# Reordering the first loads of an attention kernel, and one transpose ahead of a step's scores

## The chip, the cores and the metric

The kernel runs on one core of a Trainium2 chip. The metric is the device time of one execution in microseconds (us); lower is better. Most executions agree within 0.3%. All times inside an execution are us from the start of its span.

## The reference

```python
xn = layernorm(x)                                   # x: 1 x 2048 x 512
q  = (xn @ wq)                                      # 32 heads of 128
p  = softmax(q @ k_cache.T * 128**-0.5)             # 2048 keys a head
s  = (p @ v_cache) @ wo
g  = silu(relu(xn @ w1 + b1)**2 @ w2 + b2)
out = x + s * g
```

## The kernel before

The tensor engine (PE) does the matmuls and some transposes (its weight loads are listed as PEld), ACT the exponentials, DVE and POOL the rest; SP sends nearly all transfers. Queries are taken in four blocks of 512, which are four tiles of 128 rows each. Block 0, head 0 has a start of its own: K of head 0 comes as two plain halves that PE transposes, each x tile is normalised, transposed on PE and projected, and scores are made tile by tile, so that ACT can begin early. A step of head 0 is one tile of queries against one half of the keys: its scores (queries times K), its exponential, and its PV (the exponentials times V).

```python
def ln_load(j, i, eng=SP):      # x tile i of block j: 128 KB
    t_xl[jt] = S.emit_dma(eng, partial(_dma, out=x_ln[:, i, :], in_=...), sl_xl[i], deps=[...])

def load_k0(b):                 # half b of K, head 0: 256 KB, by SP
    ...
def k0_transpose(b):            # 8 PE transposes; waits for that half
    ...
def first_transpose(i):         # 4 PE transposes of normalised tile i
    ...
def first_proj(i):              # 4 matmuls with wq of head 0
    ...
# --- the loads, in program order of each engine ---
ln_load(0, 0, SP)
ln_load(0, 1, AC)
load_k0(0)
fill_wq(0, AC)                  # wq of head 0: 128 KB in rows of 256 bytes
load_k0(1)
E(AC, partial(_act, out=th_t[:, 0, 0:1], in_=warm[:, 0:1], func=ACT.Exp), deps=[t_warm])
ln_load(0, 2, SP)
ln_load(0, 3, SP)
fill_wq(1); load_v0(0); load_v0(1)
...
# --- the work, in program order of each engine ---
warm_up(36)
k0_transpose(0); k0_copy(0)
ln_bn(0, 0); ln_rstd(0, 0, eng=DV); ln_bn(0, 1); ln_scale(0, 0)
first_transpose(0)
k0_transpose(1); k0_copy(1)
...
first_copy(0); first_proj(0); ...
first_transpose(1)
gen_scores(0); ...              # gen_scores and gen_pv are steps of head 0
gen_pv(0)
ln_bn(0, 3, 0, HD)
gen_scores(2)
ln_scale(0, 2)
first_transpose(2)
ln_bn(0, 3, HD, D)
gen_scores(3)
first_copy(2)
...
```

PE works strictly in this order: the first x transposes stand behind the transposes of K's first half, and the first projection behind those of K's second half.

The softmax here doesn't subtract the row's maximum and nothing guards it: scores larger than these inputs give would overflow.

## Time and profile before

| | before |
|---|---|
| time, median of the 3 runs | 1238.17 us (1237.9 to 1238.31) |
| span of the profiled execution | 1236.1 us |
| first scores start | 7.58 us |
| weights of head 1's first scores start | 16.59 us |
| from there to the end | 1219.5 us |

The prediction shows the busy table, the chain of waits and the issue rows. The timeline of PE, with columns start, duration, engine, line, operation, tiles, count, and in brackets the idle time before it and what ended that:

```profile
4.86 0.73 PE L196 MATMUL psO<-ident,kT 128*128 128x128 bf16 x8
...
5.95 0.61 PE L196 MATMUL psO<-ident,kT 128*128 128x128 bf16 x8
6.72 0.38 PE L152 MATMUL psF<-xnT,wq_sb 128*128 128x128 bf16 x4 [0.16 <-DVE xnT L179]
```

The reader is to see that the projection waits for the copy of the x tile. The view of transfers, cut to the issue of each K half (last column: us from issue to landing):

```profile
kT<-in_A_k_cache_dram SPq DMA_DIRECT2D x1, 256.0 KB, 3.6
...
kT<-in_A_k_cache_dram SPq DMA_DIRECT2D x1, 256.0 KB, 4.2
```

Issued at 1.18 and 1.64, the halves land at 4.82 and 5.85. The first is not early enough, though the timeline shows no wait: it counts the last warm-up matmul as busy until 5.00. That matmul starts at 4.69, and the warm-up matmuls start 0.107 apart, so the transposes could have started at 4.80. They start at 4.86, which is 0.046 after the landing, as they do within 0.001 in twelve of the fourteen traces. That cost nothing yet: they end near 5.43, and PE then waits for the normalised x tile until 5.71. Nor does the second set hold anything: it ends near 6.40, and the projection starts at 6.72. An estimate from these starts: the first half could have come 0.29 later, and the second 0.37 later, before tile 0 had to wait for K.

### The profile page before, as it was taken

Reading aid. Unit: us, or ns where it says so; the run is one execution under the profiler, and the core shown is the slowest. Engines: PE = TensorE matmul, PEld = TensorE weight load, DVE = VectorE, ACT = ScalarE, POOL = GpSimd, SP = SyncE. Lnnn points to the kernel's source line nnn. Section 1 sums busy time; section 2 is a strip of 40 time slices with the busy share of each in tenths; the row PEclk is TensorE's granted clock in tenths of the full one; section 3 lists DMA queues with packets and bytes.
Section 4 is the critical chain, followed back from the end, with each engine's and each line's share of the span. In section 5 each row is a group of like instructions: output and inputs, shape, how many; then the busy total and the mean of one; then the engine's idle time right before and its main releaser. Section 6 shows DMA issues by size and latency. Waiting matters only on the chain.

```text
span 1236.1 us, 26728 instructions
## 1 busy us (share of the span) xinstructions
PE 1220.8 (99%) x11678; PEld 819.1 (66%) x11885; DVE 472.8 (38%) x953; ACT 1054.6 (85%) x1044; POOL 32.0 (3%) x73
## 2 busy tenths in 40 slices
PE   9999999999999999999999999999999999999998
PEld 7666666666666666666666666666666666666665
DVE  4453323244435332334444532333344333324333
ACT  7888888888888888888888888888888888888885
POOL 1010000000002000000000200000000000000000
PEclk9999999999999999999999999999999999999999
DMA  9999998787879897768779878787778788878771
GB/s 211 203 245 194 187 178 134 130 144 143 140 152 171 144 158 129 141 138 144 133 135 169 171 138 144 141 148 133 134 146 148 146 154 158 137 134 146 145 124 31
DMA packets 686868, 185.41 MB, mean 150 GB/s; under 512 B 673536, under 2 KB 685568, under 8 KB 686752
## 3 DMA queue, kind: packets, MB, share of 16 engines
q1 hardware_dynamic: 684656, 179.62, 80.0%
q0 software_dynamic: 1424, 3.81, 1.2%
q8 instruction: 94, 1.54, 0.6%
q10 hardware_dynamic: 672, 0.26, 0.1%
q14 instruction: 22, 0.18, 0.0%
HBM read 96.60 MB, written 2.10 MB: 80 GB/s over the span
## 4 chain that ended last, share of the span: by engine, by line
PE 98%; issue 1%; DVE 0%; DMA 0%; POOL 0%; DVEq 0%
PE psO L157 38%; PE psA L152 35%; PE psF L152 25%; PE psA L157 0%; DMA x_ln<-in_A_x_dram 0%; DVE out_t L165 0%; PE psF L196 0%; DVE tmp_t L175 0%; PE psO L152 0%; DVE xnT L179 0%; DVE st_t L200 0%; POOL rstd L165 0%; DVE xn_t L171 0%; DVE mv_t L204 0%; DVE ve_t L171 0%
## 5 line engine op out<-in xcount | busy, mean ns | idle before, releaser
L161 ACT ACTIVATE pT<-psA 128x1024 bf16<-128x1024 f32 x1024 | 1044.5, 1024 | 162.9 <-PE psA L152 117.6
L157 PEld LDWEIGHTS psO<-v_sb,pT 128*128 128x128 bf16 x8192 | 547.9, 98 | 240.3 <-issue 12.4
L157 PE MATMUL psO<-v_sb,pT 128*128 128x129 bf16 x8192 | 631.2, 220 | 0.5
L152 PE MATMUL psA<-qt_sb,kT 128*128 128x512 bf16 x1840 | 562.9, 379 | 10.1
L179 DVE COPY o_un<-psO 128x258 f32<-128x258 f32 x256 | 97.4, 422 | 399.5 <-PE psO L157 398.8
L152 PE MATMUL psF<-xnT,wq_sb 128*128 128x512 bf16 (+1 forms) x508 | 165.7, 374 | 0.4 <-DVE xnT L179 0.2
L152 PE MATMUL psF<-wo_all,oT 128*128 128x512 bf16 x478 | 163.2, 379 | 0.1
L152 PEld LDWEIGHTS psA<-qt_sb,kT 128*128 128x128 bf16 x2032 | 157.0, 98 | 0.0
L179 DVE CAST qt_sb<-psF 128x512 bf16<-128x512 f32 (+1 forms) x130 | 88.0, 677 | 97.3 <-PE psF L152 93.7
L165 DVE TENSOR_TENSOR o_bf<-o_un,rden 128x512 bf16<-128x512 f32 x128 | 88.6, 692 | 4.7 <-DVE rden L183 0.3
L152 PEld LDWEIGHTS psF<-xnT,wq_sb 128*128 128x128 bf16 x520 | 50.3, 98 | 60.0 <-issue 0.3
L171 DVE TENSOR_SCALAR r_t<-psF,b1f 128x512 bf16<-128x512 f32 x56 | 42.0, 750 | 117.4 <-PE psF L152 117.4
L152 PEld LDWEIGHTS psF<-wo_all,oT 128*128 128x128 bf16 x480 | 46.9, 98 | 56.4
L152 PE MATMUL psF<-xnT,w_sb 128*128 128x512 bf16 x224 | 77.1, 379 | 0.0
L152 PE MATMUL psF<-w_sb,h2T 128*128 128x512 bf16 x223 | 73.7, 379 | 0.0
L152 PEld LDWEIGHTS psF<-xnT,w_sb 128*128 128x128 bf16 x224 | 21.9, 98 | 26.4
L152 PEld LDWEIGHTS psF<-w_sb,h2T 128*128 128x128 bf16 x224 | 21.9, 98 | 26.4
L165 DVE TENSOR_TENSOR z_t<-psF,b2bc 128x512 f32<-128x512 f32 x16 | 11.1, 692 | 67.2 <-PE psF L152 62.0
L165 DVE TENSOR_TENSOR acc<-psF,acc 128x512 f32<-128x512 f32 x28 | 19.3, 689 | 30.0 <-PE psF L152 30.0
L208 POOL DMA_DIRECT2D out_dram<-out_t x12 | 6.7, 554 | 891.1 <-DVE out_t L165 891.1
L165 DVE TENSOR_TENSOR h2T<-r_t 128x512 bf16<-128x512 bf16 x56 | 23.8, 426 | 1.9
L183 DVE RECIPROCAL rden<-o_un 128x4 f32<-128x4 f32 x128 | 22.9, 179 | 4.4
(47 smaller groups left out, 165.2 us busy)
## 6 DMA issues: line engine op xcount, KB each, us to landing
v_sb<-in_A_v_cache_dram SPq DMA_DIRECT2D x127, 512.0 KB, 4.7
wq_sb<-in_A_wq_dram SPq DMA_DIRECT2D x127, 128.0 KB, 3.1
wo_all<-in_A_wo_dram SPq DMA_DIRECT2D x4, 1024.0 KB, 6.4
w_sb<-in_B_w_dram SPq DMA_DIRECT2D x14, 256.0 KB, 4.1
oT<-o_bf SPq DMA_TRANSPOSE x128, 4.0
x_t<-in_A_x_dram POOLq DMA_DIRECT2D x16, 128.0 KB, 3.5
kT<-in_A_k_cache_dram SPq DMA_TRANSPOSE x127, 4.5
x_ln<-in_A_x_dram SPq DMA_DIRECT2D x15, 128.0 KB, 4.0
```

Of the source, the lines that this page charges most:

```text
L152: return e.matmul(out, lhsT, rhs, start=start, stop=stop)
L157: return e.matmul(out, lhsT, rhs, start=start, stop=stop, skip_group_check=True)
L161: return e.activation(out, in_, func, bias=bias, scale=scale)
L165: return e.tensor_tensor(out, in0, in1, op)
L171: return e.tensor_scalar(out, in0, scalar1=scalar1, scalar2=scalar2, op0=op0, op1=op1)
L179: return e.tensor_copy(out, in_)
L183: return e.reciprocal(out, in_)
L208: return e.dma_start(out, in_)
```

## The change

The intent: x tile 0 is what the whole start waits for. In the old order it shares the DMA engines with tile 1, which ACT sends at the same moment. The new order gives SP both tiles, leaves ACT only wq, behind its table load and first activation, and moves the transpose of the third tile ahead of step 2's scores, so that the copy of that tile runs under scores.

```diff
     ln_load(0, 0, SP)
-    ln_load(0, 1, AC)
+    ln_load(0, 1, SP)
     load_k0(0)
-    fill_wq(0, AC)
     load_k0(1)
     E(AC, partial(_act, out=th_t[:, 0, 0:1], in_=warm[:, 0:1], func=ACT.Exp), deps=[t_warm])
+    fill_wq(0, AC)
...
     ln_bn(0, 3, 0, HD)
-    gen_scores(2)
     ln_scale(0, 2)
     first_transpose(2)
+    gen_scores(2)
```

## The prediction

> **What bounds the kernel now.** I read the busy table first, then the groups, then the chain of work that ended last, then the timeline of the first 20 us, because the diff touches nothing after that. All times below are us from the start of the span unless marked otherwise.
>
> ```profile
> PE 1220.8 (99%) x11678; PEld 819.1 (66%) x11885; DVE 472.8 (38%) x953; ACT 1054.6 (85%) x1044; POOL 32.0 (3%) x73
> ...
> PE 98%; issue 1%; DVE 0%; DMA 0%; POOL 0%; DVEq 0%
> ...
> L161 ACT ACTIVATE pT<-psA 128x1024 bf16<-128x1024 f32 x1024 | 1044.5, 1024 | 162.9 <-PE psA L152 117.6
> ```
>
> The tensor engine (PE) is busy 99% of the span and makes up 98% of the chain. The exponentials on ACT, the next busiest engine, sit idle for 162.9 us, mostly because they wait for the scores. So from the second head on the kernel runs at the pace of PE, and a change at its start can only move the whole stream earlier or later by a fraction of a microsecond; it cannot change the pace. Everything therefore hangs on the start. The chain cut to the first 20 us says what the start waits for:
>
> ```profile
> 0.72 2.71 DMA x_ln<-in_A_x_dram
> 3.43 0.02 issue
> 3.45 0.71 DVE st_t L200
> ...
> 4.64 0.58 POOL rstd L165
> ...
> 5.25 0.42 DVE xn_t L171
> ...
> 5.71 0.41 PE psF L196 x4
> ...
> 6.72 0.38 PE psF L152 x4
> ...
> 10.64 0.44 DVE xnT L179
> ```
>
> The first x tile takes 2.71 to land, then DVE and POOL normalise it, PE transposes it at 5.71 and projects it at 6.72. So the landing of this tile is on the path that sets the end. The 10.64 line is the other place that the diff touches: the copy of the third query tile is on the path too.
>
> A matmul of 128 columns here advances PE by 0.0557 (the chain has sixteen scores matmuls in 0.89). With that I laid the PE rows of the timeline end to end (start plus count times 0.0557, against the next start) and found these holes before 15.7: 0.40 before the first transpose at 5.71, 0.34 before its projection at 6.72, 0.14 at 7.08, 0.28 at 7.58, 0.16 at 9.30, 0.25 at 11.12, 0.12 at 12.60, 0.11 at 14.27. They sum to 1.80. **That is the ceiling:** with no hole at all in the prologue the kernel would be 1.80 of 1238.17, or 0.15%, faster. The warm-up matmuls ahead of it last until 4.86 and are not changed.
>
> **What the Trainium skill says.** "DMA: Bandwidth & Descriptors", section "Issuing engines are not separate DMA queues": transfers issued by several engines run on the same 16 DMA engines and interleave; issuing from two engines saves only issue time. The same page, "Queues, rings and completion order": a DMA engine takes turns between the queues that have work, packet by packet. The trace before fits: tiles 0 and 1 are issued at the same moment from two queues and land nearly together, after 2.7 and 2.9.
>
> ```profile
> 0.72 0.41 ACTq L208 DMA_DIRECT2D x_ln<-in_A_x_dram  x1
> 0.72 0.40 SPq L208 DMA_DIRECT2D x_ln<-in_A_x_dram  x1
> ...
> 1.16 0.46 ACTq L208 DMA_DIRECT2D wq_sb<-in_A_wq_dram  x1
> 1.18 0.89 SPq L208 DMA_DIRECT2D kT<-in_A_k_cache_dram  x2
> ...
> 1.65 1.28 ACT L161 ACT_TABLE_LOAD   x1 [1.65 <-PEq L1024]
> ```
>
> "ScalarE: Activation LUTs", section "What ACT_TABLE_LOAD costs": about 1283 ns plus a drain of about 1380 ns. The trace has the 1.28; the activation follows at 2.95, so no drain shows here. "Perfetto Trace Analysis", section "Sequencer Loop": a sequencer pushes engine instructions into a queue and goes on. If that holds, the wq transfer placed behind the table load and the activation need not wait for either; nothing in this trace decides it, as no transfer follows an activation on ACT.
>
> **Part 1, the loads.** Nothing is added or removed: the same transfers leave in another order. SP gains one issue (0.40) in second place, so every later issue of SP moves from its old time to about 0.40 later. ACT loses one and sends wq for head 0 behind the table load: at about 2.2 if the sequencer waits (0.7 + 1.28 + 0.21), at about 1.0 if it waits only for the memset of the warm tile (ended 0.92). Before, that transfer left at 1.16.
>
> What tile 0 gains: the DMA view by slices of 0.4 gives 20 KB moved by 2.0, 81 by 2.4, 220 by 2.8. Tiles 0 and 1 together are 262 KB, reached near 2.9, and tile 0 landed at 3.43, some 0.5 after. If tile 0 has the engines for itself, its 131 KB are through near 2.55, which gives a landing near 3.05: 0.4 earlier at the best. If wq is issued at 1.0 it shares the engines from about 0.3 after tile 0 started, and the gain is perhaps half. I take 0.27.
>
> Does it pass down the path? Tile 1's statistics stand between on DVE at 4.47; issued at 1.12 with 2.9 to land, tile 1 is there at 4.0, in time. The K transposes ahead of the first transpose are held by the warm-up till 4.86 and end at 5.31 (8 x 0.0557), and their K half landed at 1.18 + 3.6 = 4.78. It is issued 0.40 later now, but the engines are saturated (nine tenths or more busy from 2.4 on), so it lands by bytes moved, and the bytes ahead of it are the same or fewer: about 4.8 again. So the first transpose can go as early as about 5.35, and the room is 0.36. The second K half landed at 1.62 + 4.2 = 5.8; its transposes then fill PE from 5.85 to 6.30, while DVE copies the transposed tile, so the projection comes near 6.45 in place of 6.72. Wq landed at 1.16 + 4.0 = 5.16 before; issued at 2.2 it lands near 6.2 by the same duration, which is under 6.45, by 0.25 only. Later: scores for step 1 need the second K copy of ACT, done at 5.63 + 1.99 = 7.62; at a shift of 0.27 they start near 7.76, still free. So part 1 is worth 0.27.
>
> What SP's delay of 0.40 costs: K of head 1 was issued at 4.71 and took 8.0, so 12.7, needed at 16.86; its V 9.78 + 5.2 = 15.0, needed at 17.51; wq for head 2 9.16 + 4.0 = 13.2, needed at 17.08; V of head 0 3.54 + 4.9 = 8.4, needed at 9.30. The smallest slack is 0.9, so nothing.
>
> **Part 2, the transpose ahead of the scores.** Times as before, without part 1. The normalised third tile is there at 9.44 + 0.40 = 9.84. PE is free of the first PV at 9.75, so the transpose starts at 9.90: a new hole of 0.15 in place of none. It takes 0.22, then scores 2 and 3 take 0.45 each, to 11.02. The copy is done at 9.90 + 0.39 + 0.04 + 0.42 = 10.75, under these scores, so the projection follows at 11.02 where it stood at 11.12: a gain of 0.10. But scores 2 now end 0.35 later, so exponential 2 starts near 10.78 (was 10.41) and 3 ends near 12.72; scores 5 want that buffer and could go at 12.76, while PE would be ready at 12.59. Before they began at 12.83. So the hole of 0.12 at 12.60 goes and one of 0.17 comes, and 0.07 is what remains of the gain. ACT catches up after, since it had waited 0.88 before the exponential at 15.49. So part 2 is worth 0.07.
>
> **Sum:** 0.27 + 0.07 = 0.34, so 1238.17 - 0.34 = 1237.83, rounded to 1237.8.
>
> **The rivals.** (a) Wq for head 0 comes late and takes the place of tile 0 as what the first projection waits for. For it: issue at 2.2 behind 1.28 + 0.21 of ACT work, in rows of 256 bytes, beside a full SP queue. Against: the queue of ACT has it alone and gets its turns, and there is 0.25 of room. It would eat 0.2 to 0.7: 1237.9 to 1238.4. (b) The sequencer doesn't wait, wq leaves at about 1.0, shares the engines with tile 0 as tile 1 did, and tile 0 gains little. Then part 1 is worth 0.1: 1238.0. The skill speaks for it. (c) The first K half, issued 0.40 later, lands 0.40 later, at 5.2: its transposes end at 5.65 and the first transpose is where it was: no gain from part 1. The saturation speaks against. (d) More is gained: tile 0 gets 0.4, the hole at 9.30 shrinks too, and exponential 3 doesn't bind: 1237.4.
>
> **Range and chances.** The rivals span 1237.4 to 1238.4. The three runs before span 0.41, and a median of three can be off by 0.2 or so; that makes 1237.0 to 1238.6. More than 2%, 24.8 us, is far beyond the ceiling of 1.80, and no part of the change touches the steady stretch: 0.98 for within 2%, the rest for surprises, split evenly.
>
> **What would show it right or wrong.** In the chain of the first 20 us the x tile should read about 2.4 where it read 2.71; the first transpose should start near 5.45, its projection near 6.45. If the projection's wait names wq, rival (a) holds; the issue time of wq on ACT (2.2 or 1.0) tells (b); a first K transpose well past 4.86 tells (c). For part 2: the transpose of tile 2 waits for DVE by about 0.15, the hole before its projection is gone, and scores 5 wait for an exponential. The start of the first scores of head 1 (16.86 before) should be near 16.5, and the same shift should be found at the end. The prediction is wrong if that shift grows or vanishes after 20 us, or if the K, V or w1 loads that SP sends later hold PE between 16 and 30.

## The result, and the profile after

The changed kernel took 1238.46 us (median of 6 runs, 1237.88 to 1240.01) against 1238.02 (6 runs, 1237.9 to 1238.31) of the kernel before. The ratio is 1.0004, 95% interval 0.9991 to 1.0017: the same.

The page after, the lines that answer to those of the prediction:

```profile
PE 1231.4 (100%) x11885; PEld 818.9 (66%) x11885; DVE 472.3 (38%) x953; ACT 1053.6 (85%) x1044; POOL 32.1 (3%) x73
...
PE 99%; DMA 0%; DVE 0%; SPq 0%; issue 0%; DVEq 0%
...
L161 ACT ACTIVATE pT<-psA 128x1024 bf16<-128x1024 f32 x1024 | 1043.4, 1023 | 163.5 <-PE psA L152 118.1
```

PE's busy time seems to have grown by 10 us. It has not: the page before holds 11678 matmul records and this one 11885, while both hold 11885 weight loads. Some 200 records are missing from the trace before. What can be compared is the start of one and the same instruction, and that is how the rest is read.

The chain of waits after, cut to the first 20 us (start, duration, what):

```profile
1.65 0.42 SPq L208
...
2.11 4.13 DMA kT<-in_A_k_cache_dram
...
6.29 0.62 PE psO L196 x8
6.91 0.24 PE psF L152 x4
...
7.60 1.05 PE psA L157 x16
...
9.95 0.36 PE psF L196 x4
```

Where the chain before began with the x tile, it now begins with SP's issues one after another, and the transfer on it is the second half of K, which takes 4.13 to land, until 6.24. The first scores start at 7.60; before, at 7.58. The copy of tile 2, on the chain before at 10.64, is gone from it: the transpose at 9.95 is followed by scores. The issue rows of the timeline:

```profile
0.72 1.28 ACT L161 ACT_TABLE_LOAD   x1 [0.72 <-PEq L1024]
...
0.96 0.41 ACTq L208 DMA_DIRECT2D wq_sb<-in_A_wq_dram  x1
...
1.65 0.90 SPq L208 DMA_DIRECT2D kT<-in_A_k_cache_dram  x2
```

ACT sends wq at 0.96, in the middle of its own table load. That fits the Trainium skill's "Perfetto Trace Analysis", "Sequencer Loop": a sequencer pushes an engine instruction into a queue and goes on. SP sends the K halves at 1.65 and 2.11. Tile 0's statistics start at 3.05 (3.45 before), so the tile did gain 0.40. That start and PE (timeline), and the landings of the K halves (view of transfers, last column):

```profile
3.05 0.69 DVE L200 BATCH_NORM_STATS2 st_t<-x_ln 128x6 f32<-128x512 bf16 x1 [3.05 <-DMA x_ln<-in_A_x_dram]
...
5.18 0.62 PE L196 MATMUL psO<-ident,kT 128*128 128x128 bf16 x8 [0.19 <-DMA kT<-in_A_k_cache_dram]
5.64 0.39 PE L196 MATMUL psF<-ident,xn_t 128*128 128x128 bf16 x4
6.29 0.62 PE L196 MATMUL psO<-ident,kT 128*128 128x128 bf16 x8 [0.26 <-DMA kT<-in_A_k_cache_dram]
6.74 0.39 PE L152 MATMUL psF<-xnT,wq_sb 128*128 128x128 bf16 x4
```

```profile
kT<-in_A_k_cache_dram SPq DMA_DIRECT2D x1, 256.0 KB, 3.5
...
kT<-in_A_k_cache_dram SPq DMA_DIRECT2D x1, 256.0 KB, 4.1
```

Both K transposes now wait for their transfer, landed at 5.13 and 6.24. The first x transposes follow at 5.64, at once after the first set, though tile 0 was normalised by 5.26. The projection of tile 0 follows at 6.74, where it stood at 6.72: all that tile 0 gained is gone before its projection.

The other part of the change, the transpose of tile 2. PE and its weight loads before and after, same columns:

```profile
11.12 0.40 PE L152 MATMUL psF<-xnT,wq_sb 128*128 128x128 bf16 x4
...
12.83 0.61 PE L157 MATMUL psA<-qt_sb,kT 128*128 128x128 bf16 x8
...
16.59 0.15 PEld L152 LDWEIGHTS psA<-qt_sb,kT 128*128 128x128 bf16 x2
```

```profile
9.91 0.40 PE L196 MATMUL psF<-ident,xn_t 128*128 128x128 bf16 x4
...
11.04 0.39 PE L152 MATMUL psF<-xnT,wq_sb 128*128 128x128 bf16 x4
...
12.78 0.45 PEld L157 LDWEIGHTS psA<-qt_sb,kT 128*128 128x128 bf16 x8 [0.18 <-ACT pT L161]
12.79 0.62 PE L157 MATMUL psA<-qt_sb,kT 128*128 128x128 bf16 x8
...
16.56 0.15 PEld L152 LDWEIGHTS psA<-qt_sb,kT 128*128 128x128 bf16 x2
```

The projection of tile 2 comes 0.08 earlier though the first scores come 0.02 later; then the weights for scores 5 wait 0.18 for an exponential. From the first scores to the weights of head 1's first scores it is 16.56 - 7.60 = 8.96 us, against 16.59 - 7.58 = 9.01 before. From there to the end it is 1219.52 in both: nothing after the start changed. (The weight loads are used because the first of the two matmul records at head 1's start is missing from the trace before. The prediction's 16.86 is the second matmul; the first scores of head 1 start with the weights, near 16.6.)

### The profile page after: what moved, and what is told of

It is laid out like the page before. It is cut to its first block, busy times and chain, and to the rows that moved or that the text cites. A ratio compares the mean times of both kernels' runs of the same rounds, so it can differ in the third digit from the quotient of the medians.

```text
span 1236.1 us, 26935 instructions
## 1 busy us (share of the span) xinstructions
PE 1231.4 (100%) x11885; PEld 818.9 (66%) x11885; DVE 472.3 (38%) x953; ACT 1053.6 (85%) x1044; POOL 32.1 (3%) x73
## 4 chain that ended last, share of the span: by engine, by line
PE 99%; DMA 0%; DVE 0%; SPq 0%; issue 0%; DVEq 0%
PE psO L157 38%; PE psA L152 36%; PE psF L152 25%; DMA kT<-in_A_k_cache_dram 0%; PE psA L157 0%; DVE out_t L165 0%; SPq L208 0%; DVE tmp_t L175 0%; PE psO L152 0%; PE psF L196 0%; PE psO L196 0%; DVE qt_sb L179 0%; DVEq L119 0%
## 5 line engine op out<-in xcount | busy, mean ns | idle before, releaser
L152 PE MATMUL psA<-qt_sb,kT 128*128 128x512 bf16 x2032 | 604.3, 379 | 0.0
L152 PE MATMUL psF<-xnT,wq_sb 128*128 128x512 bf16 (+1 forms) x520 | 168.7, 374 | 0.0
```

Of the source, the lines that this page charges most:

```text
L152: return e.matmul(out, lhsT, rhs, start=start, stop=stop)
```

## The experiments

Three theories stood at the start. **Q**: a K half lands a fixed time after its issue, and what hurts is that its slot on SP is one later. **B**: wq, alone on ACT's queue and sent at 0.96, is moved ahead of K, so K lands later by the bytes ahead of it. **S**: part 1 did gain and part 2 lost it. All kernels gave correct results. This is what the fourteen traces show; "first scores", "weights h1" (weights of head 1's first scores) and "full clock" (when the granted clock of PE goes from half to full, from the trace's clock records) are starts in us.

| run | loads | tile 0 statistics | 1st K transposes | 2nd K transposes | first scores | weights h1 | difference | to the end | full clock |
|---|---|---|---|---|---|---|---|---|---|
| before | old | 3.45 | 4.86 | 5.95 | 7.58 | 16.59 | 9.01 | 1219.5 | 5.13 |
| e10_before_again | old | 3.39 | 4.79 | 6.08 | 7.75 | 16.76 | 9.01 | 1219.5 | 6.57 |
| e2_transpose_only | old | 3.43 | 4.87 | 6.02 | 7.55 | 16.50 | 8.96 | 1219.5 | 3.89 |
| e9_transpose_only_again | old | 4.13 | 5.62 | 6.72 | 8.25 | 17.21 | 8.96 | 1219.5 | 4.92 |
| after | new | 3.05 | 5.18 | 6.29 | 7.60 | 16.56 | 8.96 | 1219.5 | 4.84 |
| a5_after_again | new | 2.88 | 5.15 | 7.02 | 8.34 | 17.30 | 8.96 | 1219.5 | 4.64 |
| e12_after_third | new | 2.83 | 5.26 | 6.85 | 8.17 | 17.13 | 8.96 | 1219.5 | 4.88 |
| e1_loads_only | new | 2.85 | 5.00 | 7.16 | 8.47 | 17.48 | 9.01 | 1219.5 | 5.94 |
| e4_x1_on_act | mixed | 2.90 | 5.05 | 6.44 | 7.76 | 16.71 | 8.96 | 1219.5 | 3.67 |
| e8_before_wq_behind_k | old, wq late | 3.40 | 4.80 | 6.28 | 7.93 | 16.94 | 9.01 | 1219.5 | 7.03 |
| e3_wq_behind_k | new, wq late | 2.85 | 4.92 | 5.63 | 7.23 | 16.37 | 9.13 | 1219.5 | 3.70 |
| e6_wq_behind_k_again | new, wq late | 2.93 | 5.20 | 6.29 | 7.92 | 16.87 | 8.96 | 1219.5 | 6.09 |
| e7_wq_gated | new, wq late, ACT | 2.93 | 5.22 | 6.44 | 10.08 | 20.20 | 10.12 | 1219.5 | 6.39 |
| e11_v_on_act | as e3, V on ACT | 2.91 | 4.83 | 6.08 | 7.76 | 17.83 | 10.07 | 1219.5 | 6.80 |

The column "to the end" is the span less "weights h1". It is the same in all (1219.50 to 1219.53), so every difference between these executions is made before head 1.

**The loads alone.**

```diff
 (the changed kernel, and:)
+    gen_scores(2)
     ln_scale(0, 2)
     first_transpose(2)
-    gen_scores(2)
```

> The loads' new order alone, the transpose of tile 2 where it was. Theory Q (what tile 0 gains is given back because the K halves of head 0 leave SP one slot later, and land that much later): tile 0's statistics start at 3.05, first K transposes at 5.17, second at 6.29, first scores at 7.60, all as in the changed kernel; weights of head 1's first scores at 16.61 to 16.63 (16.59 before, 16.56 changed): slightly worse than before. Rival S (part 1 does gain, and it is lost again in part 2): first scores clearly before 7.58 and head 1's weights near 16.3.

One run: 1238.79 us, above all 7 runs of before on that chip (1237.83 to 1238.12). S falls: the loads alone gain nothing. But the second K transposes start at 7.16, not 6.29 as with the same loads in the changed kernel, and that is nearly the whole difference in span between the two (1237.0 and 1236.1). The landing of K varies from execution to execution; none of the theories had said so, and Q's figures for this run (7.60 and 16.61) are missed too. It became a fourth, **V**: with the new loads the second K half is late by an amount that changes from run to run, more than with the old.

**The transpose alone.**

```diff
 (the kernel before, and:)
-    gen_scores(2)
     ln_scale(0, 2)
     first_transpose(2)
+    gen_scores(2)
```

> The transpose of tile 2 moved ahead of step 2's scores alone, loads as before. Theory: a gain of its own of 0.05 to 0.07: projection of tile 2 at 11.02 (11.12 before), scores 5 waiting for an exponential and starting at 12.77 (12.83 before), weights of head 1's first scores at 16.53 to 16.55 (16.59 before). Rival: no gain alone, 16.59.

> The transpose moved alone, loads as before, again. In all traces so far the time from the first scores to head 1's weights is 9.01 with the old transpose order and 8.95 to 8.96 with the new, and from there to the end 1219.5 whatever the kernel. Theory: here 8.95 again, K halves ready by 4.9 and 6.0, median 0.0 to 0.1 below before's, spread under 0.5 as before's. Rival: the gain of 0.06 was chance, 9.01.

The first run took 1237.8 us against 1237.86. In its trace the difference is 8.96 in place of 9.01, the projection of tile 2 comes at 10.99 and scores 5 at 12.73. The second series of 5 has a median of 1237.85 (1237.79 to 1238.56) against 1238.12, ratio 0.9999 (0.9987 to 1.0012): not resolved by the times. The traces do resolve it. All four with the old place of the transpose have 9.01; all seven with the new place in which nothing else waits have 8.96. **Part 2 is worth 0.05 us.** What the second expectation said of K (ready by 4.9 and 6.0) missed: this profiled execution had all its first loads late, tile 0 at 4.13, the K halves at 5.57 and 6.67. The old order is not free of bad executions either. In both traces, with the old loads, PE waits for K's first half: by 0.33 in the first, where it landed at 4.82 but full clock had ended the warm-up sooner, and by 0.61 in the second. The line of the first:

```profile
4.87 0.62 PE L196 MATMUL psO<-ident,kT 128*128 128x128 bf16 x8 [0.33 <-DMA kT<-in_A_k_cache_dram]
```

**wq behind K, by SP.**

```diff
 (the changed kernel, and:)
     load_k0(1)
+    fill_wq(0, SP)
     E(AC, ...)
-    fill_wq(0, AC)
```

> The changed kernel, with wq of head 0 sent by SP behind both K halves in place of by ACT. Tells two causes of the late K apart. Q (a K half lands a fixed 3.5 to 4.1 after its own issue, and its slot on SP is what moved): K transposes still at 5.15 and 6.25 as in the changed kernel; wq, issued near 2.55, lands near 6.6. B (wq, alone on ACT's queue from 0.96, takes turns from the K halves): with wq gone behind them the first K transposes start at 4.86 (end of the warm-up) and the second near 5.85.

> The run with wq behind the K halves on SP, again. Theory B (wq's bytes ahead of K are what holds K): second K transposes again near 5.65, head 1's weights near 16.4, median 1237.6 to 1237.8, under before's by 0.1 to 0.3, spread under 0.6. If only chance made that run good, K is late again in this trace (6.2 or more) and the median is above before's.

PE of the first of the two (timeline):

```profile
5.63 0.62 PE L196 MATMUL psO<-ident,kT 128*128 128x128 bf16 x8
6.38 0.38 PE L152 MATMUL psF<-xnT,wq_sb 128*128 128x128 bf16 x4
...
9.28 0.39 PE L157 MATMUL psO<-v_sb,pT 128*128 128x129 bf16 x4 [0.32 <-DMA v_sb<-in_A_v_cache_dram]
```

The view reports no wait before the second K transposes, and the first scores come at 7.23, the earliest of all traces. K was issued as late as in the changed kernel, so for the second half Q falls and B holds. The first PV then waits 0.32 for V, which SP now sends one slot later, so some of the gain goes at once: 1237.67 us against 1237.86. In the second run the second half landed well too, at 5.81, but the rest of the forecast missed (second transposes at 6.29, head 1's weights at 16.87). The median of 5 is 1237.84 (1237.68 to 1238.28) against 1238.04, ratio 0.9999 (0.9985 to 1.0012): a gain of 0.2 at most, which the times do not resolve. Its first scores came at 7.92; the first K half was late (5.15, no earlier than in the changed kernel) and PE ran at half clock until 6.09. So B alone does not say when the first half is complete.

**Tile 1 on ACT again, behind the activation.**

```diff
 (the changed kernel, and:)
-    ln_load(0, 1, SP)
     load_k0(0)
     load_k0(1)
     E(AC, ...)
+    ln_load(0, 1, AC)
     fill_wq(0, AC)
```

> The changed kernel with tile 1 back on ACT, behind the activation and ahead of wq, so that SP sends tile 0, then the K halves at 1.18 and 1.62 as before. Q: tile 0 lands near 3.05, K transposes start at 4.86 and 5.85, first transpose of x near 5.35, first projection near 6.4, first scores near 7.27, weights of head 1's first scores near 16.25, span some 0.3 shorter than before (0.03%, not to be told in the times). B: the K halves are later than that, since tile 1 and wq take turns from them as tile 1 and wq did before: no earlier than 4.86 and 5.9 though. If tile 0 gains only because it is alone on the engines for 0.25, it lands between 3.05 and 3.4.

```profile
5.05 0.62 PE L196 MATMUL psO<-ident,kT 128*128 128x128 bf16 x8 [0.63 <-DMA kT<-in_A_k_cache_dram]
...
6.44 0.62 PE L196 MATMUL psO<-ident,kT 128*128 128x128 bf16 x8 [0.54 <-DMA kT<-in_A_k_cache_dram]
```

This is PE's timeline. K is issued at 1.18 and 1.62 as before, tile 0 lands early, and still both halves are late, at 5.01 and 6.39 (before: 4.82 and 5.85). That is against Q for both halves, as far as one execution tells: in e9, with the old loads, they came later still. The time is 1238.24 us (4 runs, 1238.03 to 1238.65) against 1237.86, ratio 1.0004 (0.9987 to 1.002). B does not explain it either: the same bytes left the same queues, those of ACT 0.24 later than before.

**The changed kernel again, and the kernel before again** (no edit), to see how far the loads vary.

> The changed kernel again, to see how far its loads vary. The loads-only run had the same loads as the changed kernel, yet its second K half was ready at 7.1 against 6.2, and its span was 0.9 longer. Theory V: with wq early on ACT's queue the landing of the second K half varies from run to run, and the time with it: median 1238.2 to 1238.5, spread 0.8 to 2 us, while the kernel before stays within 0.5. Rival: the slow runs were chance of one chip; then the median is within 0.1 of before and the spread like that of before.

> The changed kernel, a third trace. Theory V: first K half ready at 4.95 to 5.2, second at 6.2 to 7.1, its 16 parts spread over 1.3 or more; time 1237.9 to 1238.8. If it is ready before 6.0, the lateness is chance.

> The kernel before, for a second trace of its loads. Theory V: its second K half is ready near 5.9 (between 5.7 and 6.1), its 16 parts land within 1.0 of each other, 9.01 from first scores to head 1's weights. If it is ready at 6.2 or later, late K halves are not a mark of the new load order and V falls.

```profile
7.02 0.62 PE L196 MATMUL psO<-ident,kT 128*128 128x128 bf16 x8 [1.03 <-DMA kT<-in_A_k_cache_dram]
```

This is PE in the second trace of the changed kernel: it waits 1.03 for the second K half. The series has a median of 1238.51 us (5 runs, 1237.94 to 1238.63) against 1238.04 (9 runs, 1237.83 to 1238.16), ratio 1.0003 (0.999 to 1.0015): not the rival's median within 0.1 of before, but a smaller spread, 0.69, than V had forecast. The third took 1238.45 against 1238.12, the kernel before again 1238.07. A transfer lands in 16 parts, and the trace has the time of each. Those of the second K half:

| loads | runs | first part landed | last part landed | last less first |
|---|---|---|---|---|
| old | before, e2, e10, e9 | 5.02, 5.06, 5.20, 5.79 | 5.85, 5.98, 5.89, 6.67 | 0.84, 0.92, 0.69, 0.88 |
| new | after, a5, e12, e1 | 4.83, 5.20, 4.86, 4.81 | 6.24, 6.98, 6.81, 7.11 | 1.41, 1.78, 1.94, 2.30 |
| mixed | e4 | 5.06 | 6.39 | 1.33 |
| wq behind K | e3, e6, e7, e11, e8 | 4.43, 4.51, 4.56, 4.46, 4.36 | 5.59, 5.81, 6.07, 5.49, 6.23 | 1.16, 1.30, 1.51, 1.02, 1.87 |

Two things are shown. First, with wq behind K the first part lands between 4.36 and 4.56, ahead of every other run (4.81 to 5.79): wq's bytes do count (B). The first half says the same: in e3, e6, e7 and e11 its first part lands at 3.78 to 3.87, in the four traces of the new loads at 4.11 to 4.21, though SP issues it near 1.65 in both; so Q falls for these parts. And the packets show it: with the new loads all 512 packets of wq have started before half of the first 128 K packets have, and in the four old traces at most 2. But the last part of the first half, for which PE waits, comes at 4.78 to 5.17 with wq behind K and at 4.95 to 5.22 with the new loads: hardly earlier.

Second, in all four traces of the new loads the parts land 1.4 to 2.3 apart, against 0.7 to 0.9 in all four of the old: with the new order some of the parts lag, and PE waits for the last. That is what V had forecast for e12 and e10. Of lateness alone this can't be said: by the words of the expectation for e10 ("6.2 or later"), e9, with the same old loads, counts against V at 6.67; its parts lie close together all the same. Nor is a wide spread a mark of the new order alone, as e4 and the runs with wq behind K have it too. The packets of the K rows usually take 0.084 us; the slowest took 0.61, 0.93, 0.91 and 1.06 in the four new traces, and 0.50, 0.67, 0.46 and 1.49 in the four old ones, so single slow packets occur under both. **Why the parts of some orders land more unevenly is left open.**

**wq on ACT, held until tile 1 has landed.**

```diff
 (the changed kernel, and:)
+    S.emit_wait(AC, [t_xl[1]])
     fill_wq(0, AC)
```

> The changed kernel with wq of head 0 still on ACT, but issued only when tile 1 has landed (near 3.3), so it comes behind most of K and takes no slot of SP: V of head 0 no longer lands late (8.7 in place of 9.24). Theory B: K transposes at 4.87 and 5.65, wq lands near 6.0, first scores near 7.23, first PV near 8.97 (9.28 with wq on SP), head 1's weights near 16.1, median near 1237.4, 0.4 to 0.5 under before's. If wq lands after 6.4 the first projection waits for it and the gain shrinks by the difference.

```profile
9.21 0.40 PE L152 MATMUL psF<-xnT,wq_sb 128*128 128x128 bf16 x4 [2.16 <-DMA wq_sb<-in_A_wq_dram]
...
10.08 1.86 PE L157 MATMUL psA<-qt_sb,kT 128*128 128x128 bf16 x16 [0.25 <-DVE qt_sb L179]
```

A miss; this made it worse: 1240.58 us (5 runs, 1239.11 to 1241.53), ratio 1.0018 (1.0005 to 1.003), the only one whose interval leaves 1 out. Issued at 3.51, wq needed 5.7 to land; 15 of its 16 parts were there by 8.20, the last at 9.16. PE waited 2.16, and then a second loss followed: sixteen scores matmuls take 1.86 where they take 1.05 elsewhere. The clock records show half clock from 9.80 for 3.41 us.

**The kernel before, with wq behind K.**

```diff
 (the kernel before, and:)
-    fill_wq(0, AC)
     load_k0(1)
+    fill_wq(0, SP)
```

> The kernel before with wq of head 0 sent by SP behind both K halves, tile 1 still on ACT at the start. Theory: there the x tile holds the first transpose, not K, so an earlier K brings nothing: K halves land by 4.6 and 5.5, the first transpose stays near 5.68 with its wait for DVE, first scores near 7.55, head 1's weights within 0.05 of 16.59, time within 0.1 of before. Rival: if it gains 0.2 or more, freeing K from wq is worth something with the old x order too, and the new x order is not needed.

```profile
4.80 1.06 PE L196 MATMUL psO<-ident,kT 128*128 128x128 bf16 x8
```

The time is 1238.12 us (4 runs, 1238.01 to 1238.25) against 1238.04, ratio 1.0001 (0.9987 to 1.0014): within 0.1, as forecast. The trace missed its forecasts for the second half and the first scores. The first half landed at 4.36, the earliest of all, and the first transpose stayed at 5.66, held by the x tile; but the second half landed at 6.23 and PE ran at half clock until 7.03 (1.06 for eight transposes in place of 0.62), so the first scores came at 7.93.

**V's first half on ACT, on top of wq behind K:** a try at a version that beats both kernels.

```diff
 (the changed kernel with wq behind K by SP, and:)
-    load_v0(0)
+    S.emit_wait(AC, [t_k0[0]])
+    load_v0(0, AC)
     load_v0(1)
```

> The run with wq behind both K halves on SP, and V's first half for head 0 moved to ACT's queue, issued when the first K half has landed (near 5), so that the first PV need not wait for V (9.24 there) . Theory: V's half lands near 8, first scores as in those two runs (7.2 to 7.9), first PV 1.7 after the first scores, 8.95 from the first scores to head 1's weights in place of 9.14; median 1237.3 to 1237.8, below before's by 0.2 to 0.6. Rival: a part of V lands late as wq did when ACT sent it late, and the first PV waits for it: 1238 or more.

```profile
10.75 0.44 PE L157 MATMUL psO<-v_sb,pT 128*128 128x129 bf16 x5 [1.27 <-DMA v_sb<-in_A_v_cache_dram]
```

A miss, and the rival named in the expectation: issued at 4.80, V's half took 5.8 to land, and the first PV waited 1.27 for it. The median is 1239.13 us (5 runs, 1238.89 to 1240.71) against 1238.12, ratio 1.001 (0.9997 to 1.0024). No version tried is shown to beat the kernel before by its times; the best that the traces support is the old loads with the new place of the transpose, for 0.05 us.

## Why the prediction was right or wrong

**Right:** the range, the chances for 2%, and the view of the steady stretch: it takes 1219.5 of some 1236 us of span in every trace, so the change could only move the start. That the median lies within the range is partly luck: its upper end came from rival (a), which is not what happened, and two of the six executions (1238.62 and 1240.01) lie above it. The ceiling of 1.80 bounds a gain only; the run with wq held back lost more than that. And its first hole is too large: the prediction has the first K transposes held by the warm-up and done at 5.31, but they waited for K's landing, and at half clock until 5.13 they ended near 5.43, so the hole is 0.29 and not 0.40.

**Wrong:** the gain of 0.34. The medians of the two series are 0.44 and 0.47 above before's, a loss that the intervals, which hold 1, do not resolve. By its steps:

- Tile 0 gains 0.27: **undersized.** It gained 0.40 in the profiled execution and 0.57 to 0.62 in the other three with the new loads. Rival (b) had its first half right (wq left at 0.96, the sequencer did not wait) and its conclusion wrong (tile 0 gained all the same).
- "It lands by bytes moved, and the bytes ahead of it are the same or fewer: about 4.8 again": **this is the step that failed**, along with the same for the second half ("landed at ... 5.8"). In the four traces with the new loads the first half was there at 4.95 to 5.22 and the second at 6.24 to 7.11. The bytes ahead were not fewer: wq, sent at 0.96, went ahead of K as a whole (its packets start from 2.13 to 3.10; before, from 3.42 to 4.84, among K's). Besides, the last of 16 parts decides, and when that lands no sum of bytes told; this share of the delay stays open. The outcome is that of rival (c), written off because the engines were saturated: the first K transposes end near 5.64 and the first x transposes start there (5.71 before). Its reason, the later slot on SP, is not shown: with wq out of the way K's first parts came early from the same slot. Beyond (c), the second set of K transposes then waits 0.26 to 1.03 us, and the projection stands behind it.
- The room for wq, rival (a): wq landed at 3.52 and was never in the way in the changed kernel. It became so in the run that held it back.
- SP's later issues cost nothing: held. After the second K half the chain of the first 20 us has no transfer.
- Part 2 is worth 0.07: **right, about 0.05.** By its terms: the hole ahead of the transpose is 9.91 - (9.33 + 8 x 0.0557) = 0.13 (0.15 forecast); the projection follows the scores without a hole; scores 5 wait 0.18 (0.17 forecast) for an exponential.
- Not foreseen at all: that the loads vary between executions by more than the gain sought, and the clock. PE starts at half clock (warm-up matmuls start 0.107 apart, against 0.0557 later), and full clock came anywhere from 3.67 to 7.03 in the fourteen traces. The Trainium skill has the mechanism ("TensorE: Matmul & The Clock Gate", "What's actually happening": a free-running window of 3413 ns), and the trace agrees with the window: 3.413 us of half clock in the run with wq held back. One execution of the changed kernel took 1240.01 us at a mean clock of 0.999, the same mean as in that run; that PE waited there long enough to lose its clock for one window fits, but there is no trace of that execution, so it is argued and not shown.

What part 1 costs on average is only roughly known. The mean start of the first scores is 8.15 in the four traces with the new loads (7.60, 8.34, 8.17, 8.47) and 7.78 in the four with the old (7.58, 7.75, 7.55, 8.25), so about 0.4, with overlap. Of the 11 executions of the two series of the changed kernel, 7 took longer than the slowest of before in the same rounds.

## What to carry to other kernels

When two inputs meet in one in-order queue, moving one of them ahead helps only up to the slack of the other; here K's halves had some 0.3 us of it, tile 0 came 0.4 us sooner, and the second half of K came 0.4 us later or more. Estimate a landing from its own last part and from several executions, not from bytes over bandwidth: a load that is just in time in one trace can be late in the next, as K's halves landed 0.75 and 0.82 us later in e9 than in the first trace, with the same loads. And look for a stretch of the trace that is constant across kernels (here from head 1 to the end), since then one instruction's start tells differences of 0.05 us that the times of whole executions cannot.

## What the Trainium skill lacked or had wrong

- "DMA: Bandwidth & Descriptors" has arbitration by packet, but no figure for how far apart the 16 parts of one transfer land: 0.7 to 2.3 us for 256 KB here, with single packets of 2 KB taking up to 1.49 us in place of 0.084. For a start-up path that is the number needed.
- The same page says that issuing from two engines "will only save the time on the sequencer". No run here shows that to be wrong, as none changes the queue of a transfer without its time or place; but the page has no warning that a load moved to a second queue can be issued sooner and go ahead of others: wq on ACT at 0.96 put the first part of K's first half at 4.11 to 4.21, against 3.78 to 3.87 with wq on SP behind K or held back.
- "TensorE: Matmul & The Clock Gate", "What's actually happening", puts the scatter of the transition at 500 ns to either side. In these traces full clock came between 3.67 and 7.03, 3.36 us apart, nearly the whole window.
- "ScalarE: Activation LUTs", "What ACT_TABLE_LOAD costs": 1283 ns is right (1.28 before and after), but the drain of 1380 ns does not show at a first load: the activation follows 0.02 us after it.
